# A gated mix of linear attention and a bilinear MLP: six buffers for w_down rows, attention rows loaded a unit sooner, first loads in another order

## The chip, the cores and the metric

The kernel runs on one core of a Trainium2 chip. The core has five engines with an instruction queue each, which meet only through semaphores: TensorE (PE in the profile; its weight loads are PEld) multiplies matrices, VectorE (DVE) and ScalarE (ACT) work on elements, GpSimd (POOL) here only prepares constants and issues DMAs, and SyncE (SP) issues most DMAs. Sixteen DMA engines move the data between HBM and the on-chip memory SBUF. TensorE writes to PSUM, of which the kernel uses eight tiles (banks) of 128 x 512 float32.

The metric is the device time of one execution in microseconds (us). The kernel before takes 608.49 us, the median of three runs (607.94 to 609.02).

## The reference

The input x has 2048 rows of 512. Two branches read it, and a gate per row mixes them:

```python
g = sigmoid((x * gate_w).sum(-1, keepdims=True))
a = linear_attention(x, wqkv, wo)        # 32 heads of 16
h = (x @ w_gate) * (x @ w_up)            # 2048 x 1792, no nonlinearity
b = h @ w_down
out = g * a + (1 - g) * b
```

The linear attention takes phi(t) = (t + 1 where t > 0, else exp(t)) + 1e-6 of q and k, sums kv = phi(k)^T v and z = sum of phi(k) over all rows for each head, and gives o = (phi(q) kv) / (phi(q) z + 1e-6), which is multiplied by wo. Everything is float32.

## The kernel before

**Three matmuls for one.** TensorE's fast format (float32r) keeps fewer bits than float32. So an operand is split into a high part (a rounded copy, made on ScalarE) and a low part (the difference, made on VectorE), and `mm3` issues three matmuls per product: high x high, high x low, low x high. In names the last letter tells the part: xah and xal, dh and dl, wch and wcl.

**Phase 1** reads x tile by tile (16 tiles of 128 rows), computes phi(k) and accumulates G = x^T phi(k) in PSUM. At its start all comes from HBM at once: four loads `wraw` of the key weights (`raw_load`, one of 128 rows each) and five loads `xlead` of the first four tiles of x. `wraw` is split into wkh and wkl, `xlead` into xah and xal, and the first matmul `pk<-wkh,xah` needs the first of each. TensorE meanwhile runs seven warm-up matmuls on zeros. Later tiles come as `xraw` and `xtraw`. From its sixth tile on, phase 1 also loads the first blocks of phase 2 (`cb_load` into `cbs`, three buffers): `plan(t, ...)` sets after which tile a step stands in the queues.

**Phase 2** runs over two pairs of column blocks of x (1024 rows each). For each pair there are 16 *units*: 14 for the 14 column blocks of w_gate and w_up ("f"), and two for q ("q"), at places 6 and 11. So units are numbered 0 to 31, with q at 6, 11, 22 and 27. Each unit computes two 256 x 1024 products at once by a scheme with seven products in place of eight (after Strassen and Winograd): operands are sums of blocks of x (`xc`, seven of them) and of blocks of weights (seven slots of `wr`). Products 2, 3, 4, 1, 5, 6, 7 follow one another on TensorE, into four PSUM banks Y, X, R, S; between them ScalarE copies m and cross out, and VectorE combines them. Each product is six matmuls of 128 x 512.

**The weights of a unit** come in two steps. `w_load` issues on SP a 640 KB load `wr<-in_wgu` (or in_wq). `w_add` then negates two of its blocks on ScalarE (`wr<-wr`) and issues from POOL a DMA that adds a second array from HBM onto five slots (`wr<-in_wgu_add`). `w_high` makes three copies wch on ScalarE, `w_low` three differences wcl on VectorE. In unit n, `w_high(n + 1)`, `w_low(n + 1)` and `w_add(n + 2)` run, and at its end `w_load(n + 3)`; `wr` has two buffers.

**The blocks of x for pair 1** are prepared in units 0 to 15: `cb_load`, `x_add`, `cb_split`, which writes the high and low parts to HBM (`xpark`). In unit 15, each product that has read its block for the last time lets SP load the block of pair 1 over it (`reload`): 14 loads of 512 KB, named xah<-xpark2h, xal<-xpark2l, xbh<-xpark3h and so on, in the order of the products. Unit 16 is the first to use them.

**The down projection.** An f unit leaves h split in `hh`, `hl`, and splits its rows of w_down into `dh`, `dl` (`down_tiles`, five buffers of each). Two units give eight jobs (`down_jobs`): six matmuls each into a bank `pdn`, followed by an update of `acc` on ScalarE or VectorE. A unit runs three to eight jobs from the list at four places between its products (`share`).

**The attention** of a q unit n (`attention`) goes on in the units after it. In n + 1 the terms of the denominator are written to HBM and read back, in n + 3 the reciprocal goes to HBM (`den`), and four loads `rb<-den` spread it over the heads: two at place "m" of n + 3, two at its end. In n + 3 and n + 4, `norm_high` multiplies on VectorE (`rb<-phq,rb`), ScalarE copies hh, and `norm_low` makes hl. The group then acts like two f units, with W' = kv x wo in the place of w_down. W' was computed in units 3 and 4 and parked in HBM (`wpark`); `weights` loads four tiles of 256 KB of it into buffers of dh and dl.

**What sets the order.** Nothing is scheduled: every engine runs its instructions in the order in which the program issues them (`pin`, `keep_in_program_order`). `later(n, place, fn)` adds a step to unit n at a named place; the places follow one another as e, m, c, d, t, s, r, end. The framework adds the waits. A tile pool hands out a free buffer, and its first writer waits for the last reader of the tile before. DMAs from SP use eight semaphores in turn, so in the built program the issue of a load waits for the landing of the eighth load before it.

Of the kernel before, what the change touches and what calls it, by code (L numbers as in the profile page):

```python
# [14 lines left out]
P = 128  # L15
# [28 lines left out]
def gated_mix(ctx: ExitStack, tc, xt, xp, x, wqkv, wq, wq_add, wo, wgu, wgu_add, wdn, gate_w, out):  # L44
# [12 lines left out]
    def act(dst, src, func=AF.Copy, **kw):  # L57
        pin(nc.scalar.activation(dst, src, func, **kw))  # L58
# [22 lines left out]
    def dma(dst, src):  # L81
        tc.keep_in_program_order(nc.sync.dma_start(dst, src))
# [58 lines left out]
    def w_add(n):  # L141

        if n < len(order):
            _, kind, m = order[n]
            act(raws[n][:, 5:7], raws[n][:, 0:2], scale=-1.0)
            dma_add(raws[n][:, 2:7], (wgu_add if kind == "f" else wq_add)[m])
# [32 lines left out]
    with tc.tile_pool(name="p1", bufs=2, reuse_waits="tile") as p1:  # L179
# [18 lines left out]
        def raw_load(k, by):  # L198
            pin(by.dma_start(raw_of[k], wqkv[k * P:(k + 1) * P, D:2 * D]))

        raw_load(0, nc.scalar)

        act(ezcol[:, 0:1], epsc)
        raw_load(1, nc.scalar)
        for k in range(KT):
            raw = raw_of[k]
            a = p1.tile([P, LEAD, P], F32, tag="xtraw", name="xlead", bufs=4)
            step = LEAD // 2 if k == 0 else LEAD
            for i in range(0, LEAD, step):
                sl = slice(i * P, (i + step) * P)  # L210
                dma(a[:, i:i + step].rearrange("p t c -> p (t c)"), xp[0, A1 + k // 2][:, k % 2, sl])
                if i == 0:
                    if k > 1:
                        raw_load(k, nc.sync)
                    act(wkh[:, k], raw)
                split(xa[0][:, k, sl], xa[1][:, k, sl], a[:, i:i + step].rearrange("p t c -> p (t c)"), "dve")
                if i == 0:
                    tt(wkl[:, k], raw, wkh[:, k].bitcast(F32), ALU.subtract)
# [91 lines left out]
            cbs[i] = p1.tile([P, 2, CH], F32, tag="cbs", name="cbs", bufs=3)  # L310
            x_load(cbs[i], 0, i, slice(0, 2))

        for t, i in zip((6, 7, 9, 10, 12), (4, 1, 6, 7, 3)):
            plan(t, lambda i=i: cb_load(i))
            plan(t + 2, lambda i=i: x_add(cbs[i], 0, i, slice(0, 2)))
            plan(t + 5, lambda i=i: split(*xc[i], cbs.pop(i)))
# [48 lines left out]
    def later(n, place, fn):  # L365
        at.setdefault((n, place), []).append(fn)

    def do(n, place):
        for fn in at.pop((n, place), []):
            fn()  # L370
# [16 lines left out]
    def unit(n, quad):  # L387

        wh, wl = wcs.pop(n)
        bank = {t: psum.tile([P, CH], F32, tag=t, name=f"b{t}") for t in "YXRS"}  # L390

        def reload(i):
            if n + 1 == units:
                for src, part in zip(xpark[i], xc[i]):
                    dma(part.bitcast(F32), src)

        def product(i, to, start=False):
            for k in range(2):
                ks = slice(k * P, (k + 1) * P)
                mm3(bank[to], (wh[:, SLOT[i], ks], wl[:, SLOT[i], ks]), [v[:, k] for v in xc[i]],  # L400
                    start and k == 0, k == 1, not start)
            reload(i)

        m2 = p2.tile([P, CH], F32, tag="t", name="m2")
        cross = p2.tile([P, 2, CH], F32, tag="cross", name="cross")
        product(2, "Y", True)
        act(m2, bank["Y"])
        product(3, "X", True)

        tt(bank["R"], bank["X"], m2, ALU.subtract)  # L410
        do(n, "e")
        many = share(n)
        down(many[0])
        product(4, "Y")
        act(cross[:, 0], bank["Y"])
        do(n, "m")
        do(n, "c")
        down(many[1])
        do(n, "d")
        product(1, "R")  # L420
        t = p2.tile([P, CH], F32, tag="t", name="t")
        tt(t, bank["R"], cross[:, 0], ALU.add)
        if n:
            w_high(n + 1)
        w_add(n + 2)
        do(n, "t")
        product(5, "X")
        tt(bank["S"], t, bank["X"], ALU.subtract)
        act(cross[:, 1], bank["X"])
        if n:  # L430
            w_low(n + 1, 0)
        down(many[2])
        if quad:
            quad(1, 0, cross[:, 0])
        if n:
            w_low(n + 1, 1)
        do(n, "s")
        down(many[3])
        w_low(n + 1, 2)
        if quad:  # L440
            quad(0, 1, cross[:, 1])
        product(6, "R")
        if quad:
            quad(1, 1, bank["R"])
        else:
            hh, hl = hidden()
            tt(cross[:, 1], bank["R"], cross[:, 1], ALU.mult)
            act(hh[:, 1], cross[:, 1])
        do(n, "r")
        product(7, "S")  # L450
        if quad:
            quad(0, 0, bank["S"])
        else:
            tt(cross[:, 0], bank["S"], cross[:, 0], ALU.mult)
            act(hh[:, 0], cross[:, 0])

            for c in 1, 0:
                def low(c=c):
                    tt(hl[:, c], cross[:, c], hh[:, c].bitcast(F32), ALU.subtract)

                if n + 1 == len(order):
                    later(n, f"low{c}", low)
                else:
                    low()
            return hh, hl

    def hidden():
        return [p2.tile([P, 2, CH], F32R, tag=f"h{v}", name=f"h{v}", bufs=NH) for v in "hl"]

    def down_tiles():  # L470
        return [p2.tile([P, D], F32R, tag=f"d{v}", name=f"d{v}", bufs=NH) for v in "hl"]


    att = {}
# [51 lines left out]
    def down_jobs(pair, group, col):  # L526

        def job(i):
            t = pair * TPP + i
            c, sl = divmod(i, CH // P)  # L530
            sl = slice(sl * P, (sl + 1) * P)
            s = col[:, t:t + 1]
            first = (pair, i) not in acc
            if first:
                acc[pair, i] = p2.tile([P, D], F32, tag="acc", name="acc", bufs=8)
            else:
                left[pair, i] -= 1
            ends = not left[pair, i]

            step = D // 2 if ends and pair and i == TPP // 2 - 1 else D  # L540
            for o in range(0, D, step):
                cols = slice(o, o + step)
                banks.reverse()
                pd = psum.tile([P, D], F32, tag=banks[0], name="pdn", bufs=2)[:, 0:step]
                for j, ((hh, hl), w2) in enumerate(group() if callable(group) else group):
                    mm3(pd, (hh[:, c, sl], hl[:, c, sl]), [v[:, cols] for v in w2], j == 0, j == 1)
                a = acc[pair, i][:, cols]
                if first:
                    act(a, pd, scale=s)
                else:  # L550
                    stt(a, pd, s, a, ALU.mult, ALU.add)
                if ends:
                    to = nc.gpsimd if pair == 0 else nc.sync
                    tc.keep_in_program_order(to.dma_start(out[t * P:(t + 1) * P, cols], a))

        return [lambda i=i: job((i + TPP // 2) % TPP) for i in range(TPP)]


    def attention(pair, j, n):
        phs, group = {}, {}  # L560
        den = {}
        turns = n + 5 == units

# [37 lines left out]
        def norm(i):  # L601
            r, c = parts[i]
            if r not in group:
                group[r] = (hidden(), None)
            rb = p2.tile([P, CH], F32, tag="z", name="rb", bufs=4)
            one = there[HB * i:HB * (i + 1)].rearrange("h c t -> h (c t)")
            dma(rb, one[:, None, :].to_broadcast([HB, DH, CH]))
            den[i] = rb

        def norm_high(i):  # L610
            r, c = parts[i]
            stt(den[i], phs[r, c], EPS, den[i], ALU.add, ALU.mult)
            act(group[r][0][0][:, c], den[i])

        def norm_low(i):
            r, c = parts[i]
            hh, hl = group[r][0]
            tt(hl[:, c], den[i], hh[:, c].bitcast(F32), ALU.subtract)

        def weights():  # L620
            for r in range(2):
                d = down_tiles()
                for src, part in zip(wpark[2 * j + r], d):
                    dma(part.bitcast(F32), src)
                group[r] = (group[r][0], d)

        def last():

            where = len(jobs) if turns else 0
            jobs[where:where] = down_jobs(pair, lambda: [group[0], group[1]], gcol)  # L630

        for i in range(4):
            later(n + 1, "e", lambda i=i: z_part(i))
# [8 lines left out]
        for i, places in enumerate((((n + 3, "r"), (n + 4, "e")), ((n + 4, "m"), (n + 4, "c")),  # L642
                                    ((n + 4, "d"), (n + 4, "t")), ((n + 4, "s"), (n + 4, "r")))):
            for fn, (m, place) in zip((norm_high, norm_low), places):
                later(m, place, lambda i=i, fn=fn: fn(i))
        later(*((n + 5, "e") if turns else (n + 4, "c")), weights)
        later(n + 4, "end", last)
        return quad

# [121 lines left out]
```

## Time and profile before

| what | value |
| --- | --- |
| median of three runs | 608.49 us |
| the profiled execution | 606.16 us |
| its span, first to last instruction | 604.4 us |
| granted TensorE clock | 1.000 |
| PE busy | 598.9 us, 99% of the span |
| VectorE, ScalarE busy | 443.9 us (73%), 295.3 us (49%) |
| HBM read and written | 92.54 MB, 18.09 MB |
| DMA packets, mean rate | 111.13 MB, 184 GB/s |
| first matmul after the warm-up | 5.11 us |
| units 0, 15, 16, 31 start | 93.1, 312.3, 328.6, 562.7 us |

The profiled execution is one of its own, and its time is 2.33 us under the median of the three runs. Its span leaves out 1.8 us around the instructions. Matmuls are pipelined: a matmul is shown as 0.39 us long, but the next starts 0.227 us after it. In a timeline line, the brackets at the end give how long the engine stood idle before, and what ended that. DMA share is the mean busy share of the sixteen DMA engines.

### The profile page before, as it was taken

To read this page: it belongs to the slowest core of one execution; us is meant where nothing else is said; L and a number is where in the kernel's file an instruction comes from. 1 tells how busy PE (TensorE), PEld (TensorE's weight loads), DVE (VectorE), ACT (ScalarE), POOL (GpSimd) and SP (SyncE) were. 2 spreads that over 40 slices of the span, in tenths; PEclk is the share of its full clock that TensorE was granted. 3 is DMA by queue.
4 is the path that set the end of the run, shared out by engine and by line. 5 is a ranking of instruction groups with operands and counts; after the bars stand their busy time and mean duration, and the time that the engine had idled before them with its cause. 6 is when DMAs were issued, how large, how long until landed. Compare 5 with 4: busy or idle time off the path is not lost.

```text
span 604.4 us, 7537 instructions
## 1 busy us (share of the span) xinstructions
PE 598.9 (99%) x2657; PEld 494.2 (82%) x2657; DVE 443.9 (73%) x695; ACT 295.3 (49%) x507; POOL 46.3 (8%) x62
## 2 busy tenths in 40 slices
PE   8999999999999999999999999999999999999997
PEld 6888888888888888888888888888888888888886
DVE  6977896676776798867888666456677886668874
ACT  3855765466548543564445143553473444633310
POOL 0011100001111100110100021000000000000000
PEclk9999999999999999999999999999999999999999
DMA  8576956677868967888779975444487456552313
GB/s 290 188 212 125 293 171 161 171 186 213 226 176 203 304 162 221 239 207 235 195 189 341 384 208 170 104 106 104 89 218 174 129 176 137 175 135 63 103 35 140
DMA packets 49702, 111.13 MB, mean 184 GB/s; under 512 B 4736, under 2 KB 13952, under 8 KB 49664
## 3 DMA queue, kind: packets, MB, share of 16 engines
q1 hardware_dynamic: 41968, 81.80, 40.2%
q0 software_dynamic: 7408, 28.32, 25.2%
q10 hardware_dynamic: 288, 0.52, 0.3%
q8 instruction: 21, 0.34, 0.2%
q14 instruction: 17, 0.14, 0.1%
HBM read 92.54 MB, written 18.09 MB: 183 GB/s over the span
## 4 chain that ended last, share of the span: by engine, by line
PE 99%; DMA 1%; ACT 0%; DVE 0%; issue 0%
PE pdn L52 32%; PE bY L52 14%; PE bR L52 14%; PE bX L52 14%; PE pk L52 7%; PE gt L52 7%; PE bS L52 7%; DMA wraw<-in_wqkv 1%; PE pkv L52 1%; PE pw L52 0%; PE pz L52 0%; ACT wkh L58 0%; DVE acc L64 0%
## 5 line engine op out<-in xcount | busy, mean ns | idle before, releaser
L52 PE MATMUL pdn<-dl,hh 128*128 128x512 f32 x290 | 112.4, 388 | 0.0
L52 PE MATMUL pdn<-dh,hh 128*128 128x512 f32 x290 | 112.4, 388 | 0.0
L52 PE MATMUL pdn<-dh,hl 128*128 128x512 f32 x290 | 112.4, 388 | 0.0
L58 ACT ACTIVATE hh<-cross 128x512 fp32r<-128x512 f32 x56 | 35.1, 633 | 98.2 <-DVE cross L61 98.2
L64 DVE SCALAR_TENSOR_TENSOR acc<-pdn,ocol,acc 128x512 f32<-128x512 f32 (+1 forms) x97 | 71.4, 739 | 14.9 <-PE pdn L52 13.5
L61 DVE TENSOR_TENSOR wcl<-wr,wch 128x512 fp32r<-128x512 f32 (+1 forms) x96 | 72.9, 772 | 0.0
L52 PEld LDWEIGHTS pdn<-dl,hh 128*128 128x128 f32 x290 | 54.4, 188 | 11.3
L52 PEld LDWEIGHTS pdn<-dh,hh 128*128 128x128 f32 x290 | 54.4, 188 | 11.2
L52 PEld LDWEIGHTS pdn<-dh,hl 128*128 128x128 f32 x290 | 54.4, 188 | 11.1
L58 ACT ACTIVATE wch<-wr 128x512 fp32r<-128x512 f32 (+1 forms) x96 | 60.2, 693 | 1.0 <-DMA wr<-in_wgu_add 1.0
L58 ACT ACTIVATE cross<-bY 128x512 f32<-128x512 f32 x32 | 19.1, 598 | 73.8 <-PE bY L52 60.1
L61 DVE TENSOR_TENSOR dl<-wdr,dh 128x512 fp32r<-128x512 f32 x28 | 19.4, 692 | 44.0 <-ACT dh L58 44.0
L52 PE MATMUL bX<-xbl,wch 128*128 128x512 f32 x128 | 49.9, 390 | 0.0
L52 PE MATMUL bX<-xbh,wch 128*128 128x512 f32 x128 | 49.8, 389 | 0.0
L52 PE MATMUL bX<-xbh,wcl 128*128 128x512 f32 x128 | 49.8, 389 | 0.0
L85 POOL DMA_DIRECT2D wr<-in_wgu_add x28 | 24.2, 865 | 293.4 <-ACT wr L58 138.7
L61 DVE TENSOR_TENSOR hl<-cross,hh 128x512 fp32r<-128x512 f32 x56 | 37.8, 688 | 2.7
L61 DVE TENSOR_TENSOR bR<-bX,m 128x512 f32<-128x512 f32 x32 | 22.3, 698 | 17.3 <-PE bX L52 17.3
L58 ACT ACTIVATE cross<-bX 128x512 f32<-128x512 f32 x32 | 19.1, 596 | 31.1 <-DVE bS L61 31.1
L61 DVE TENSOR_TENSOR bS<-t,bX 128x512 f32<-128x512 f32 x32 | 22.2, 695 | 14.0 <-PE bX L52 13.8
L64 DVE SCALAR_TENSOR_TENSOR acc<-pdn,gcol,acc 128x512 f32<-128x512 f32 x32 | 23.8, 749 | 10.9 <-PE pdn L52 10.7
L61 DVE TENSOR_TENSOR t<-bR,cross 128x512 f32<-128x512 f32 x32 | 22.0, 686 | 10.9 <-PE bR L52 10.9
(151 smaller groups left out, 1257.3 us busy)
## 6 DMA issues: line engine op xcount, KB each, us to landing
wr<-in_wgu SPq DMA_DIRECT2D x28, 640.0 KB, 5.7
wr<-in_wgu_add POOLq DMA_DIRECT2D x28, 640.0 KB, 7.1
wdr<-in_wdn SPq DMA_DIRECT2D x28, 256.0 KB, 2.9
xraw<-in_x SPq DMA_DIRECT2D x16, 256.0 KB, 6.2
terms<-zq SPq DMA_DIRECT2D x16, 256.0 KB, 2.2
zt<-terms SPq DMA_DIRECT2D x16, 256.0 KB, 6.3
rb<-den SPq DMA_DIRECT2D x16, 256.0 KB
cbs<-in_xp SPq DMA_DIRECT2D x14, 256.0 KB, 6.0
```

Source lines behind the costliest of these rows:

```text
L52: tc.keep_in_program_order(nc.tensor.matmul(*args, **kw))
L58: pin(nc.scalar.activation(dst, src, func, **kw))
L61: pin(nc.vector.tensor_tensor(dst, a, b, op=op))
L64: pin(nc.vector.scalar_tensor_tensor(dst, a, scalar, b, op0=op0, op1=op1))
L85: tc.keep_in_program_order(nc.gpsimd.dma_start(dst, src, accum_op=ALU.add))
```

## The change

The change has five parts.

- *Buffers.* `down_tiles` has six buffers (NH + 1), `cross` two. The room comes from the descriptor scratch, of which the program reserves 8192 bytes per partition in place of the framework's default of 16384.
- *W' rows.* `weights` stands in unit n + 3 at place "c" for all four groups. Before, it stood in unit n + 4 at "c", and for the group of unit 11 in unit n + 5 = 16 at "e". On SP's queue the four loads of unit 6's group now stand after xpark1l and before cbs, wr and the last two rb loads; those of unit 11's group after xpark7l and before wr, two rb loads and the fourteen reloads.
- *w_add.* It stands ahead of product 1 in its unit: on ScalarE the negation is now ahead of the three copies of `w_high`.
- *First loads.* `xlead` is read from the array xt, in pieces of 128 columns, not from xp. The second `wraw` goes from ACT's queue to SP's, and the tiny activation on ezcol is gone.
- *Phase 1.* One cb_load moves from tile 10 to 11, with its x_add and its split.

TensorE's instructions and their order stay the same.

```diff
         raw_load(0, nc.scalar)
-
-        act(ezcol[:, 0:1], epsc)
-        raw_load(1, nc.scalar)
         for k in range(KT):
...
-                dma(a[:, i:i + step].rearrange("p t c -> p (t c)"), xp[0, A1 + k // 2][:, k % 2, sl])
+                dma(a[:, i:i + step], xt[i:i + step, :, k, :].rearrange("t p c -> p t c"))
                 if i == 0:
-                    if k > 1:
+                    if k:
                         raw_load(k, nc.sync)
...
-        for t, i in zip((6, 7, 9, 10, 12), (4, 1, 6, 7, 3)):
+        for t, i in zip((6, 7, 9, 11, 12), (4, 1, 6, 7, 3)):
...
-        cross = p2.tile([P, 2, CH], F32, tag="cross", name="cross")
+        cross = p2.tile([P, 2, CH], F32, tag="cross", name="cross", bufs=2)
...
         do(n, "d")
+        w_add(n + 2)
         product(1, "R")
         t = p2.tile([P, CH], F32, tag="t", name="t")
         tt(t, bank["R"], cross[:, 0], ALU.add)
         if n:
             w_high(n + 1)
-        w_add(n + 2)
...
-        return [p2.tile([P, D], F32R, tag=f"d{v}", name=f"d{v}", bufs=NH) for v in "hl"]
+        return [p2.tile([P, D], F32R, tag=f"d{v}", name=f"d{v}", bufs=NH + 1) for v in "hl"]
...
-        later(*((n + 5, "e") if turns else (n + 4, "c")), weights)
+        later(n + 3, "c", weights)
...
-    nc = bacc.Bacc("TRN2", target_bir_lowering=False, num_devices=1)
+    nc = bacc.Bacc("TRN2", target_bir_lowering=False, num_devices=1, dynamic_dma_scratch_size=8192)
```

The rest of the diff hands the group and its W' tiles to `down_jobs` in another form.

More of the change, by code (lines that the diff above doesn't have):

```diff
@@ L559, in attention @@
     def attention(pair, j, n):
-        phs, group = {}, {}
+        phs, group, wrow = {}, {}, {}
         den = {}
@@ L603, in norm @@
             if r not in group:
-                group[r] = (hidden(), None)
+                group[r] = hidden()
             rb = p2.tile([P, CH], F32, tag="z", name="rb", bufs=4)
@@ L612, in norm_high @@
             stt(den[i], phs[r, c], EPS, den[i], ALU.add, ALU.mult)
-            act(group[r][0][0][:, c], den[i])
+            act(group[r][0][:, c], den[i])
         def norm_low(i):
             r, c = parts[i]
-            hh, hl = group[r][0]
+            hh, hl = group[r]
             tt(hl[:, c], den[i], hh[:, c].bitcast(F32), ALU.subtract)
@@ L621, in weights @@
             for r in range(2):
-                d = down_tiles()
-                for src, part in zip(wpark[2 * j + r], d):
+                wrow[r] = down_tiles()
+                for src, part in zip(wpark[2 * j + r], wrow[r]):
                     dma(part.bitcast(F32), src)
-                group[r] = (group[r][0], d)
         def last():
             where = len(jobs) if turns else 0
-            jobs[where:where] = down_jobs(pair, lambda: [group[0], group[1]], gcol)
+            jobs[where:where] = down_jobs(pair, [(group[r], wrow[r]) for r in range(2)], gcol)
         for i in range(4):
```

## Prediction

> **What bounds the kernel now.** I read the page first: the span, the share of each engine, the chain.
>
> ```profile
> span 604.4 us, 7537 instructions
> PE 598.9 (99%) x2657; PEld 494.2 (82%) x2657; DVE 443.9 (73%) x695; ACT 295.3 (49%) x507; POOL 46.3 (8%) x62
> PE 99%; DMA 1%; ACT 0%; DVE 0%; issue 0%
> ```
>
> TensorE is busy for 99% and is the chain. Then its waits, all there are:
>
> ```profile
> PE warm L52 <- DVE epsc L111: 1.3, 1, 1.3
> PE pk L52 <- ACT wkh L58: 0.8, 1, 0.8
> ```
>
> After 5.11 us a matmul starts every 0.227 us, down to the last at 600.71. So the change can save only what lies ahead of 5.11, and some tenths inside; anything that comes late adds in full. The question is which supplies are already just in time. TensorE's timeline shows two places:
>
> ```profile
> 251.88 0.39 PE L52 MATMUL pdn<-dh,hl 128*128 128x512 f32 x1
> 252.31 0.50 PE L52 MATMUL bY<-xc4h,wch 128*128 128x512 f32 x1
> ...
> 341.11 0.48 PE L52 MATMUL bX<-xbl,wch 128*128 128x512 f32 x1
> 341.43 0.39 PE L52 MATMUL bX<-xbh,wcl 128*128 128x512 f32 x1
> ```
>
> At 252.31 (unit 11) a matmul starts 0.43 after the one before it: 0.2 us were lost. At 341.11 (unit 16) a weight load needed the reloaded xbl, and 0.1 was lost. Both have no spare at all. Next, the timeline of SP, which issues the loads, around the second:
>
> ```profile
> 307.91 0.38 SPq L82 DMA_DIRECT2D xpark7l<-cbs  x1
> 311.45 0.33 SPq L82 DMA_DIRECT2D wr<-in_wgu  x1
> ...
> 313.88 0.33 SPq L82 DMA_DIRECT2D xah<-xpark2h  x1
> ...
> 329.86 0.32 SPq L82 DMA_DIRECT2D xbl<-xpark5l  x1
> ...
> 337.39 0.33 SPq L82 DMA_DIRECT2D wr<-in_wgu  x1
> 338.62 0.32 SPq L82 DMA_DIRECT2D dh<-wpark2h  x1
> ...
> 341.06 0.32 SPq L82 DMA_DIRECT2D dh<-wpark3h  x1
> ```
>
> A load on SP waits until the eighth one before it has landed, so dh<-wpark3h goes out at 341.06 because xbl, eight before it, landed then: 11 us after its issue. The queue is full. By stretches (PE, PEld, DVE, ACT, POOL; clock, DMA share, GB/s):
>
> ```profile
> 307.00:311.00 4.00, 4.00 (x20) 3.30 (x19) 3.83 (x6) 0.60 (x1) 0.86 (x1) 1.00 0.61 156
> 333.00:346.00 13.00, 13.00 (x59) 10.59 (x58) 8.53 (x13) 2.89 (x5) 0.00 (x0) 1.00 1.02 403
> ```
>
> From 311 to 346 the DMA engines are at a share of 1.0 to 1.06. What the change puts into this queue ahead of xbl makes TensorE late.
>
> **The change part by part.** *W' rows sooner.* Each of the four attention groups loads four tiles dh, dl of 256 KB, 1.05 MB. For unit 11's group they now stand in unit 14 at place "c", right behind xpark7l (307.91), and so ahead of wr, the last two rb loads and all 14 reloads; before they stood at 338.62 to 342.34, behind them. Their buffers were last read by jobs that ended before 301.4, so they go out at once. Price: 1.05 MB at the 403 GB/s of 333 to 346 is 2.6 us; at the 306 GB/s of 316 to 323 it is 3.4, the upper end. The lower: 307 to 311 shows a share of 0.61, so 0.39 x 4 us x 403 = 0.63 MB might slip in unseen, leaving 0.42 MB, 1.0 us. I take 2.6: two rb loads are ahead, and while they run the share stays near 0.6 with work queued (0.59 from 226 to 231), so half of the engines have no gap to fill, and a load lands with its slowest engine. [...]
> xbl has no spare, so TensorE waits 2.6 us at unit 16's product 5 (0.5 of it already at product 3, whose xbl had 2 us of spare). The later reloads, with 2 us or more of their own, follow that delay and add nothing.
>
> The group of unit 6 moves from unit 10 to unit 9, behind xpark1l (227.46), ahead of cbs, wr and the last two rb (236.54). The third rb decides:
>
> ```profile
> 241.98 0.69 DVE L64 SCALAR_TENSOR_TENSOR rb<-phq,rb 128x512 f32<-128x512 f32 x1 [0.40 <-DMA rb<-den]
> ```
>
> VectorE waited for it, then ran without a break to 253.7. Its product of bS at 250.43 releases these on ScalarE, and m releases the matmul at 252.31:
>
> ```profile
> 251.14 0.63 ACT L58 ACTIVATE hh<-cross 128x512 fp32r<-128x512 f32 x1 [0.56 <-DVE cross L61]
> 251.68 0.58 ACT L58 ACTIVATE m<-bY 128x512 f32<-128x512 f32 x1
> ```
>
> Every us by which rb lands later is one for TensorE. Bounds: 2.6, all bytes ahead of it, and 0, all hidden, as 231 to 237 has a share of 0.85. Of the 2.6 some 0.4 fits near 236, where the share falls to 0.27 for 1 us; I take 2.2.
>
> In pair 1 the two groups move the same way, but the DMA engines have room (a share of 0.37 in 560 to 574) and VectorE never waits for an rb: bounds 0 and 1, I take 0.
>
> *w_add sooner.* ScalarE's negation (0.63, queue pace 0.53) and the POOL add move ahead of w_high's three copies (1.88). In some 30 units the copies start 0.53 later; they end 2.9 us or more before the next unit reads them (245.11 against 248.03 at the least): 0. But the negation waits for its 640 KB load, and now the copies, the move of bX and the next unit's w_low on VectorE are queued behind it. Loads that landed after the copies' start: 211.3 against 208.97, 256.4 against 255.03, 290.2 against 289.6, 461.3 against 459.2; all within the spare. And one that is not, unit 16:
>
> ```profile
> 336.66 1.88 ACT L58 ACTIVATE wch<-wr 128x512 fp32r<-128x512 f32 x3
> 347.63 0.63 ACT L58 ACTIVATE wr<-wr 128x512 f32<-128x512 f32 x1 [9.10 <-DMA wr<-in_wgu]
> ```
>
> The copies for unit 17 now come after 347.63. Negation 0.53, copy one and two 1.15, then VectorE's two subtractions, with an acc update between, 2.0: the low half is ready 3.2 to 3.7 later, at 351.0. TensorE wants it at its third matmul of unit 17, 349.16 + 0.45 = 349.6: 1.3 us. If the load comes s later, so does TensorE by the first step, and 1.3 stands. Bounds 0.5 and 2.
>
> *First loads.* xlead comes from xt in pieces of 512 B (terms, of that size, run at 343 GB/s, the first loads at 381): 1.05 MB, 0.3 us more, under a spare of 1 to 2 us in the first projections. The start is set by the first wraw (in the chain from 0.80 for 3.61, so landed at 4.41), still alone at the head of ACT's queue. Bounds: 0.9 saved (a start at 4.2, where the warm-up ends) and 0.4 lost; I take 0. The dropped 0.20 activation stood in idle time.
>
> *At nothing:* cb load at 11 (SP's wait from 39.94 to 58.56 now comes behind one more xtraw; VectorE's split moves by 3 us, and its work ahead of the last g matmuls is the same sum); two cross tiles (ScalarE's waits there end on bY, 60.1, and bS, 31.1, not on old readers); six buffers (TensorE never waits on dh, dl); the smaller scratch (POOL has at most two DMAs out).
>
> **Sum.** 2.2 + 2.6 + 1.3 = 6.1 us. The profiled execution took 606.16, of which 1.8 lie around the span; so 612.3 there. It was 2.33 under the median of 608.49: predicted 614.6.
>
> **The rivals.** *Not slower: the W' rows are hidden.* They fill the share of 0.39 (307 to 311) and 0.41 (226 to 231) left by rb, xbl and rb land as before, and the early negation finds its load sooner: 608.5. It decides if the shift at xbl stays under 0.1 us; against it speaks the 0.63 MB that fits at most. [...]
> *Half hidden:* 1.0 at xbl, 0.8 at rb and 1.3: 611.6.
> *Only the negation costs:* 1.3, 609.8.
> *More late than counted:* behind the negation bX and the acc updates also hold PSUM banks; TensorE could lose a further 2 to 4 us in unit 17: 616.6 to 618.6.
> *Faster:* the start comes at 4.2 and the tenths at 93 to 119, 252 and 341 (0.85 together) go: 606.7. It needs the first wraw to land 0.9 sooner, and every other step to be wrong.
>
> **How the numbers follow.** What a measurement can tell from no change is 0.2%, 1.2 us. All three stalls 0.42 (614.6); half hidden 0.22; negation alone 0.07, on the border, half of it slower; more than counted 0.10; hidden 0.12; faster 0.07. Slower: 0.42 + 0.22 + 0.035 + 0.10, rounded 0.78; same 0.15; faster 0.07. The range from 608.0 to 616.6 leaves out faster and most of "more than counted", 0.17.
>
> **What would show it.** TensorE's waits should have new lines: bY (unit 11) on ScalarE's m, near 254.5; bX on the xbl load, near 344; unit 17's first product on wcl or wch. SP should issue xah<-xpark2h near 317 and each reload 2.6 later against its unit's start. ScalarE's wait for in_wgu should stand ahead of wch. First matmul at 5.1. If no such wait stands there, the W' bytes were hidden and I am wrong.

## The result, and the profile after

The changed kernel takes 614.22 us, the median of six runs (613.12 to 616.3); the kernel before took 608.22 in the six runs beside them (607.05 to 609.5). The ratio is 1.0102, with a 95% interval of 1.008 to 1.0124: slower by 1%, 6.0 us. (The ratios here are those on record with their intervals; they differ by up to 0.15% from the quotients of the medians.) Predicted were 614.6 us. The total came out right; of its parts only some did, as the following shows.

The page of the changed kernel's profiled execution (613.99 us), its span, busy engines and chain:

```profile
span 612.3 us, 7533 instructions
...
PE 602.4 (98%) x2657; PEld 494.6 (81%) x2657; DVE 443.3 (72%) x695; ACT 294.8 (48%) x506; POOL 46.4 (8%) x62
...
PE 81%; DMA 9%; DVE 5%; issue 2%; ACT 1%; SPq 1%; DVEq 0%; ACTq 0%
```

The chain that was 99% TensorE now runs for 9% of the span through DMAs: somewhere TensorE stood behind a load. Its waits (us in total, times, longest):

```profile
PE bX L52 <- DMA xbl<-xpark3l: 2.9, 1, 2.9
PE warm L52 <- DVE xc1h L109: 1.3, 1, 1.3
PE bY L52 <- ACT m L58: 1.2, 1, 1.2
PE pk L52 <- ACT wkh L58: 0.6, 1, 0.6
PE gt L52 <- DVE xnl L61: 0.4, 1, 0.4
```

Two were predicted (bX on an xbl, bY on m), one was not (gt on xnl), and of unit 17's wcl there is nothing. TensorE's timeline at the largest:

```profile
332.54 0.39 PE L52 MATMUL bY<-xah,wcl 128*128 128x512 f32 x1
332.83 0.47 PE L52 MATMUL bX<-xbh,wch 128*128 128x512 f32 x1
336.20 0.80 PE L52 MATMUL bX<-xbl,wch 128*128 128x512 f32 x1 [2.90 <-DMA xbl<-xpark3l]
336.79 0.63 PE L52 MATMUL bX<-xbh,wcl 128*128 128x512 f32 x1
337.21 0.63 PE L52 MATMUL bX<-xbh,wch 128*128 128x512 f32 x1
```

This is product 3 of unit 16, not product 5. And after the wait the next matmuls start 0.427 us apart, not 0.227: from 336.2 to 338.9 each takes nearly twice its time. By stretches (PE, PEld, DVE, ACT, POOL; clock, DMA share, GB/s) the clock explains it:

```profile
333.00:336.00 3.00, 0.30 (x1) 0.00 (x0) 3.00 (x6) 0.64 (x2) 0.00 (x0) 0.94 1.10 263
336.00:339.00 3.00, 2.80 (x7) 2.25 (x8) 1.44 (x3) 1.11 (x2) 0.00 (x0) 0.50 1.00 348
339.00:342.00 3.00, 3.00 (x15) 2.48 (x14) 1.55 (x3) 0.00 (x0) 0.00 (x0) 0.99 1.04 416
```

The granted clock falls to 0.50 at 335.67, near the end of the idle time, and stays there until 339.08: six matmuls with 0.2 us extra each and a part of a seventh, 1.3 us on top of the wait.

**Where all of it went.** TensorE runs the same 2657 matmuls in the same order in every kernel of this study, so the n-th matmul can be compared across traces. The table gives, for each profiled execution, how much more time TensorE took over a stretch than in the first profile of before (us). The stretches end at the matmuls that in that profile start at 80, 130, 260, 346, 352 and 601 us; the first holds the start of the first real matmul too. All fourteen traces are in it; the kernels are told of below.

| profiled execution | head, to 80 | phase 1's end | units 3 to 11 | units 11 to 16 | unit 17's start | pair 1 | sum |
| --- | --- | --- | --- | --- | --- | --- | --- |
| before | 0 | 0 | 0 | 0 | 0 | 0 | 0 |
| before, again | -0.1 | 0.0 | 2.2 | 0.4 | 0.0 | 0.0 | 2.5 |
| changed | 0.4 | 0.65 | 1.3 | 5.0 | 0.25 | 0.3 | 7.9 |
| changed, again | 0.5 | 0.7 | 3.2 | 4.3 | 0.0 | 1.3 | 10.0 |
| W' late | -0.2 | 0.6 | 1.5 | -0.1 | 1.34 | 0.0 | 3.1 |
| W' of 11 late | 0.4 | 0.6 | 1.6 | 0.1 | 1.41 | 0.2 | 4.4 |
| add late | 0.55 | 0.7 | 1.3 | 3.0 | 0.0 | 0.0 | 5.5 |
| before + W' | -0.1 | 0.0 | 1.9 | 3.2 | 0.0 | 0.15 | 5.1 |
| before + add | 1.9 | 0.2 | 1.9 | 0.3 | 1.35 | 0.0 | 5.6 |
| before + W' + add | 2.4 | 0.1 | 1.2 | 2.35 | 1.32 | 1.55 | 9.0 |
| before + first loads | 0.1 | 0.0 | 1.25 | 0.6 | 0.0 | 0.0 | 1.95 |
| before + copied block | 1.9 | 0.6 | 0.0 | 0.2 | 0.0 | 0.15 | 2.8 |
| before, rb first | 1.7 | -0.1 | -0.4 | 0.0 | 0.0 | 0.0 | 1.2 |
| rb and first loads | 0.05 | -0.1 | -0.4 | 0.0 | 0.0 | 0.0 | -0.4 |

A single profile is one draw. The next part begins with that. The stretch of units 3 to 11 goes by one load. VectorE starts on the third rb once it has landed, at 241.98 in the first profile of before; how much later it starts in another trace, TensorE's own lateness at 130 us taken off, is the loss of that stretch within 0.1 us in ten traces. (The others are "before + add", told of below, and the two with the rb loads moved.)

### The profile page after: what moved, and what is told of

Its sections match the earlier page's. It is cut to its first block, busy times and chain, and to the rows that moved or that the text cites. A ratio compares the mean times of both kernels' runs of the same rounds, so it can differ in the third digit from the quotient of the medians.

```text
span 612.3 us, 7533 instructions
## 1 busy us (share of the span) xinstructions
PE 602.4 (98%) x2657; PEld 494.6 (81%) x2657; DVE 443.3 (72%) x695; ACT 294.8 (48%) x506; POOL 46.4 (8%) x62
## 4 chain that ended last, share of the span: by engine, by line
PE 81%; DMA 9%; DVE 5%; issue 2%; ACT 1%; SPq 1%; DVEq 0%; ACTq 0%
PE pdn L52 27%; PE bX L52 12%; PE bY L52 12%; PE bR L52 12%; PE pk L52 7%; PE bS L52 6%; PE gt L52 5%; DMA xbl<-xpark3l 2%; DMA rb<-den 2%; DMA dh<-wpark3h 1%; DMA wr<-in_wgu 1%; SPq L82 1%; DVE wcl L61 1%; DMA wraw<-in_wqkv 1%; DMA den<-den 1%
## 5 line engine op out<-in xcount | busy, mean ns | idle before, releaser
L61 DVE TENSOR_TENSOR bR<-bX,m 128x512 f32<-128x512 f32 x32 | 22.3, 698 | 16.2 <-PE bX L52 16.1
L52 PEld LDWEIGHTS bX<-xbl,wch 128*128 128x128 f32 x128 | 24.3, 190 | 8.2 <-DMA xbl<-xpark3l 3.2
```

Source lines behind the costliest of these rows:

```text
L52: tc.keep_in_program_order(nc.tensor.matmul(*args, **kw))
L61: pin(nc.vector.tensor_tensor(dst, a, b, op=op))
```

## The experiments

**1. Is the first profile of before a usual one?** Its 606.16 us lie below all other runs of that kernel (606.34 to 612.86 over the runs of this study, medians 608.2 to 608.95). Both kernels were profiled again, unchanged.

> The kernel before, unchanged, profiled a second time: its 606.16 us lie below nearly all of its other runs. Theory (the just-in-time loads vary from run to run): own time 607.5 to 610, and TensorE's wait on ScalarE's m in unit 11 grown from 0.2 to about 1.2 us, as the third rb lands later after the same queue. Rival (the head varies): unit 11 as before, but more matmuls at 0.427 us after 5.1. A third: own time near 606.2 and no new wait, so that what differs lies outside the trace.

Measured: 608.58 us, span 606.9. Of TensorE's waits, the two that lie in phase 2:

```profile
PE bY L52 <- ACT m L58: 1.8, 1, 1.8
...
PE bX L52 <- DMA xbl<-xpark5l: 0.2, 1, 0.2
```

The wait that the prediction charged to the change, bY on ScalarE's m in unit 11, stands there in the kernel before, 1.8 us of it. SP and VectorE around the third rb load of this second profile:

```profile
236.47 0.37 SPq L82 DMA_DIRECT2D wr<-in_wgu  x1
236.90 1.25 SPq L82 DMA_DIRECT2D rb<-den  x2
...
244.08 0.69 DVE L64 SCALAR_TENSOR_TENSOR rb<-phq,rb 128x512 f32<-128x512 f32 x1 [2.58 <-DMA rb<-den]
```

In the first profile the same load was issued at 236.54 and VectorE went on at 241.98 after 0.40 us. The same program, the same queue ahead of it, 0.36 us later in issue, and the load took 7.2 us where it had taken 5.4. So the first profile was a lucky one by 2 us in this place.

> The changed kernel, unchanged, profiled a second time. Theory: unit 16's one wait on xbl<-xpark3l comes again, 2.5 to 3.5 us, and where TensorE is idle for 3 us or more the granted clock is 0.5 for some 2.7 us behind it (1.5 us lost); unit 17 under 0.4; unit 11 waits 1 to 2 us, as the kernel before does in its second profile. Own time 613 to 616. Rival (the drop of the clock was an accident of that execution): the wait of 3 us without a clock of 0.5, 612.5.

Measured: 616.18 us, 0.2 above the expected range. The wait on xbl<-xpark3l came again:

```profile
PE bY L52 <- ACT m L58: 2.8, 2, 1.8
PE bX L52 <- DMA xbl<-xpark3l: 2.4, 1, 2.4
...
PE bR L52 <- DVE t L61: 1.1, 1, 1.1
PE gt L52 <- DVE xnl L61: 0.4, 1, 0.4
```

and so did the clock's drop, after a shorter gap than expected: 2.83 us from one matmul's start to the next's.

```profile
337.00:338.00 1.00, 0.74 (x3) 0.65 (x4) 0.90 (x3) 0.85 (x2) 0.00 (x0) 0.93 1.08 264
338.00:341.00 3.00, 3.00 (x8) 2.32 (x8) 1.21 (x2) 0.27 (x1) 0.00 (x0) 0.50 0.99 391
```

Here it falls a little after the restart, at 337.86, and holds for 3.41 us, eight matmuls and 1.6 us lost. Unit 17 lost nothing, as expected; that pair 1 lost 1.3 us (the second wait of bY on m, at 512.69) was not. The wait of bR on t stands at the end of unit 10 and has the cause of unit 11's: VectorE stood 3.33 us for the third rb and so came late with t.

**2. Which part makes the stalls?** The four loads of W' and the early add were undone one at a time.

```diff
-        later(n + 3, "c", weights)
+        later(*((n + 5, "e") if turns else (n + 4, "c")), weights)
```

(The jobs then fetch the W' tiles when they run, as before. The old place of unit 11's group is the start of unit 16; the expectation says unit 15.)

> The changed kernel with its W' loads back at their old places (unit 10 and 15), all else as changed. Theory (the W' bytes ahead of rb and xbl make both stalls): the waits on ScalarE's m in unit 11 (1.1 us) and on xbl in unit 16 go, with them the stretch after 336.2 at a granted clock of 0.50; TensorE's last start 6.3 us sooner than in the changed kernel, 608 to 609.5 us, within 0.2% of before. Rival (the early add of POOL does it): TensorE still waits 2 us or more in unit 16, 611.5 to 613.

Measured: 609.08 us, ratio to before 1.0002 (0.9985 to 1.002).

```profile
PE bY L52 <- ACT m L58: 1.2, 1, 1.2
PE bY L52 <- DVE wcl L61: 0.7, 1, 0.7
PE gt L52 <- DVE xnl L61: 0.4, 1, 0.4
```

The time is as the theory said and unit 16's stall is gone, with the clock's drop. But unit 11's wait stays, against the expectation: the W' loads are not needed for it. And a new line appears, bY on wcl, in unit 17. With the matmuls next to it that wait costs 1.34 us: the 1.3 that the prediction gave the negation, which the changed kernel doesn't show.

Only the group of unit 11 at its old place. (The text below counts that of unit 27 with it, but `turns` holds for unit 11 alone, so the groups of 6, 22 and 27 all stay a unit sooner.)

```diff
-        later(n + 3, "c", weights)
+        later(*((n + 5, "e") if turns else (n + 3, "c")), weights)
```

> The changed kernel with the W' loads of units 6 and 22 sooner, those of units 11 and 27 at their old places. Theory: unit 11's wait stays at 1.1 us, unit 16's goes with the 0.50 clock: 5.2 us less than the changed kernel in the trace, 609 to 610.2 us. Rival (the early add): unit 16's wait stays above 2 us, 612 to 613.

Measured: 610.43 us, ratio 1.0024 (1.0005 to 1.0044), 0.2 above the theory's range. Unit 16 stands free again (0.1), unit 17 loses 1.41. Its median lies 1.35 above that of the kernel with all W' late. In twelve runs each on one chip that is more than noise (1.4 us between the means, 95% interval 0.8 to 2.0): the W' loads of units 6, 22 and 27 cost something. Where, the two traces don't tell: the stretch with unit 11 differs by 0.15 only, pair 1 by 0.24, and the head by 0.65, which is a draw.

The negation and the POOL add back behind w_high:

```diff
-        w_add(n + 2)
         product(1, "R")
...
             w_high(n + 1)
+        w_add(n + 2)
```

> The changed kernel with the negation and the POOL add back behind w_high. Theory (bytes of W' are the cause): unit 11's 1.1 stays; unit 16 still waits on xbl, 2.4 to 2.9 us, as only the add's bytes (0.64 MB, of which a part) leave the way; the clock's drop may go if the wait is shorter; unit 17's 0.24 goes: 611.5 to 613.5 us. Rival (the early add does it): unit 16's wait under 1 us and no drop, 609.5 to 610.5.

Measured: 611.97 us, ratio 1.0058 (1.0036 to 1.0081): the time is as the theory said, the one wait of 2.4 to 2.9 us isn't there.

```profile
PE bX L52 <- DMA xbl<-xpark3l: 1.2, 1, 1.2
PE bY L52 <- DMA xc4l<-xpark4l: 0.8, 1, 0.8
...
PE bX L52 <- DMA xbl<-xpark5l: 0.2, 1, 0.2
```

W' alone makes unit 16 late, but now in three shorter waits, at products 3, 4 and 5, and no clock drops. The same from the other side, before with only the W' loads moved (with six buffers and the smaller scratch):

```diff
-        later(*((n + 5, "e") if turns else (n + 4, "c")), weights)
+        later(n + 3, "c", weights)
```

> The kernel before with only the W' loads a unit sooner (and the six buffers and the smaller scratch that this needs). Theory: the third rb 1.1 us later, so 1.1 lost at unit 11; xbl late by 2.4 to 3.4 at unit 16, with 0 to 1.5 more for a clock of 0.5 behind it: 611.7 to 614.2 us. The lower end is without the clock's drop, as the POOL add of unit 17's weights is issued later again. Rival (the early add does it): 1.1 at unit 11 and under 1 at unit 16, 609.3 to 610.3.

Measured: 612.53 us, ratio 1.005 (1.0032 to 1.0068), inside the theory's range; 3.2 us at unit 16, at products 3 and 4:

```profile
PE bX L52 <- DMA xbl<-xpark3l: 1.4, 1, 1.4
...
PE bY L52 <- DMA xc4l<-xpark4l: 1.2, 1, 1.2
```

So of the changed kernel's 5.0 and 4.3 us there, some 3 come with the W' bytes alone; the rest comes in that kernel only with the early add beside them, as one long wait in place of the short ones, and the clock behind it.

**3. The early add alone, and both parts on the kernel before.** The add:

```diff
+        w_add(n + 2)
         product(1, "R")
...
             w_high(n + 1)
-        w_add(n + 2)
```

> The kernel before with only the negation and the POOL add moved ahead of w_high. Theory: unit 17 waits 1.3 us for wcl (as with the W' loads late), unit 16 nothing; unit 11 waits 1.2 for m if the early add delays the rb loads, 0.2 if not. Against the profile of before 1.3 to 2.5 us, so 607.5 to 608.7 there; the median over the runs, where before has part of unit 11's wait already, 609.3 to 610.5 us. Rival (the negation finds its load there and costs nothing): 608.5 to 609.2, no wait on wcl.

Measured: 610.66 us, 0.2 above the theory's range, ratio 1.0017 (0.9993 to 1.004): the rival's "costs nothing" is not shut out by the time, but by the trace, where unit 17 loses 1.35 us on wcl as the theory said. Unit 11's loss, 1.9 us, has here another wait, which was in no theory: TensorE waits 1.6 us for dh<-wpark1h, W' rows at their old place. So a late W' is not free either.

The same edit together with that of "before + W'":

> The kernel before with both the W' loads and the negation with its POOL add sooner, first loads and copied block as before. Theory (the add's bytes stand ahead of the late xbl): one wait of 2.5 to 3.4 us on xbl<-xpark3l at unit 16's product 3, with the clock's drop where TensorE is idle for 3 us, none at product 4, and under 0.4 us left at unit 17: 613 to 615 us. Rival (the two parts add up): products 3 and 4 lose 3.1 together as with the W' loads alone, and unit 17 loses 1.3 as with the add alone; about 613.3.

Measured: 614.67 us, ratio 1.0092 (1.0066 to 1.0118).

```profile
PE bX L52 <- DMA xbl<-xpark3l: 0.8, 1, 0.8
PE bY L52 <- DVE wcl L61: 0.7, 1, 0.7
PE bY L52 <- DMA xc4l<-xpark4l: 0.7, 1, 0.7
```

The time is in the theory's range, but the trace takes the rival's side: products 3 and 4 wait a little each (2.35 together), and unit 17 loses its 1.32. What differs from the changed kernel's one long wait can be seen in how long the reloads took, from issue to landing. The POOL add moves 640 KB. The DMA queues of the changed kernel (packets, MB, share of the 16 engines) in the 4 us before its bytes move, 329 to 333, and in the 4 us in which they do, 333 to 337; q1 is SP's queue, q0 the add's:

```profile
q1 hardware_dynamic: 482, 1.67, 102.3%
...
q0 software_dynamic: 128, 0.63, 78.2%
q1 hardware_dynamic: 155, 0.39, 27.7%
```

The add does not stand in line behind the reloads; while it runs, SP's queue moves a quarter of what it did. The first reload that it catches takes 2 to 4 us longer than before, and those behind it up to 5:

| kernel | add issued | xbl, product 3 | xc4h | xc4l | add gets ahead of |
| --- | --- | --- | --- | --- | --- |
| before | 326.05 | 12.4 us | 11.9 | 12.0 | none of these |
| before + W' | 329.71 | 12.5 | 13.0 | 15.4 | xc4l |
| add late | 330.40 | 12.5 | 13.0 | 15.2 | xc4l |
| before + W' + add | 329.57 | 12.5 | 15.9 | 15.0 | xc4h |
| changed | 329.00 | 14.4 | 16.6 | 16.1 | xbl |
| changed, again | 330.15 | 14.2 | 16.4 | 15.9 | xbl |

xbl was issued 7.3 and 7.15 us ahead of the add in the changed kernel's two profiles, 7.15 in the kernel with both parts, 8.7 with W' alone. It looks as if a near tie decides whether the add goes ahead of xbl or of xc4h; what tips it between the changed kernel and this one isn't settled (this one has one cross buffer and the old first loads).

**4. The two small parts that were costed at nothing.** The copied block's load, step 11 for 10:

```diff
-        for t, i in zip((6, 7, 9, 10, 12), (4, 1, 6, 7, 3)):
+        for t, i in zip((6, 7, 9, 11, 12), (4, 1, 6, 7, 3)):
```

> The kernel before with only one copied block's load moved from step 10 to step 11 of phase 1. Theory: its split stands between xnl's operations, so the last g matmuls wait 0.4 to 0.5 us for xnl near 90 us; 609.2 to 609.6 us. Rival (that wait belongs to the changed head): no wait on xnl, 608.9 us.

Measured: 609.74 us, ratio 1.001 (0.9988 to 1.0031): the effect is too small for the time; in the trace the wait of gt on xnl is there, 0.63 us with its neighbours. It belongs to this part: all six traces with the load at 11 lose 0.6 to 0.7 there, all with it at 10 lose 0.2 or less. VectorE in the changed kernel (first block) and before (second):

```profile
82.45 0.69 DVE L61 TENSOR_TENSOR xnl<-xraw,xnh 128x512 fp32r<-128x512 f32 x1 [1.05 <-ACT xnh L58]
...
84.88 1.22 DVE L61 TENSOR_TENSOR xal<-cbs,xah 128x1024 fp32r<-128x1024 f32 x1
...
86.62 0.69 DVE L61 TENSOR_TENSOR xnl<-xraw,xnh 128x512 fp32r<-128x512 f32 x1
...
89.03 1.22 DVE L61 TENSOR_TENSOR xbl<-cbs,xbh 128x1024 fp32r<-128x1024 f32 x1
...
90.17 0.69 DVE L61 TENSOR_TENSOR xnl<-xraw,xnh 128x512 fp32r<-128x512 f32 x1
```

```profile
82.56 0.68 DVE L61 TENSOR_TENSOR xnl<-xraw,xnh 128x512 fp32r<-128x512 f32 x1
...
85.58 0.68 DVE L61 TENSOR_TENSOR xnl<-xraw,xnh 128x512 fp32r<-128x512 f32 x1
...
88.00 1.21 DVE L61 TENSOR_TENSOR xbl<-cbs,xbh 128x1024 fp32r<-128x1024 f32 x1
...
89.13 0.68 DVE L61 TENSOR_TENSOR xnl<-xraw,xnh 128x512 fp32r<-128x512 f32 x1
```

The xal split has moved from ahead of 82 to 84.88, between the last xnl. The work is the same sum, but it has left a place in which VectorE then stands idle (1.05 at 82.45), and the last xnl comes 1.04 later.

The first loads:

```diff
-        act(ezcol[:, 0:1], epsc)
-        raw_load(1, nc.scalar)
...
-                dma(a[:, i:i + step].rearrange("p t c -> p (t c)"), xp[0, A1 + k // 2][:, k % 2, sl])
+                dma(a[:, i:i + step], xt[i:i + step, :, k, :].rearrange("t p c -> p t c"))
                 if i == 0:
-                    if k > 1:
+                    if k:
```

> The kernel before with only the first loads changed. Theory: first projection matmul at 4.53 instead of 5.11, and 0.3 to 0.75 us given back at once, in a wait for k = 1's wkh (second wraw behind three xleads on SP) or in matmuls at 0.427 us, since the clock is granted later than the start; no wait on xnl near 90; 608.3 to 609.2 us, within 0.2% of before. Rival (a start 0.58 sooner is a gain): 608.0 to 608.4 and TensorE's phase 1 ends 0.5 sooner.

Measured: 608.35 us, ratio 0.9991 (0.9969 to 1.0013): within 0.2% as expected. The first matmul starts at 4.53 instead of 5.11, and in this trace the matmuls right behind it start 0.566 and 0.42 apart. (In the changed kernel's first profile there is a wait too, the 0.6 on wkh: the second wraw, now on SP behind three xlead loads, landed at 7.47.) Across all fourteen traces this part turns out better than expected. TensorE's timeline of the kernel with only the copied block changed, so with the old first loads:

```profile
4.95 1.22 PE L52 MATMUL pk<-wkh,xah 128*128 128x512 f32 x2 [0.52 <-ACT wkh L58]
5.97 1.05 PE L52 MATMUL pk<-wkh,xal 128*128 128x512 f32 x2
6.82 1.05 PE L52 MATMUL pk<-wkl,xah 128*128 128x512 f32 x2
7.67 1.05 PE L52 MATMUL pk<-wkh,xah 128*128 128x512 f32 x2
8.53 0.97 PE L52 MATMUL pk<-wkh,xal 128*128 128x512 f32 x2
```

Pairs of 1.05 us are matmuls at 0.427, for 0.227 at full rate: the array is at about half its rate until 9 us, and the head loses 1.9 us. With the old first loads the head column holds 0, -0.1, -0.1, 1.7, 1.9, 1.9 and 2.4, a mean of 1.1; with the new ones -0.2, 0.05, 0.1, 0.4, 0.4, 0.5 and 0.55, a mean of 0.3. So they are worth some 0.8 us on average, by seven traces against seven, with single traces up to 2.5 us apart. The runs of the two kernels of part 5, which differ by these loads alone, agree: 1.1 us between the means, 0.2 to 2.0. The likely reason, an estimate from the starts in the traces, is the shorter pause behind the warm-up (0.74 to 0.87 us between starts, against 1.1 to 1.3). The traces' records of the granted clock fit it: full clock begins at 4.58 to 6.96 us in all seven traces with the new loads; with the old ones it begins at 4.03 to 4.20 in three, ahead of the pause's end, and not before 8.80 to 10.44 in the other four. No run changes the pause alone.

The six buffers, the smaller scratch and the two cross tiles were not run alone. The kernel with W' late has all of them, and at a ratio of 1.0002 no cost of theirs shows.

**5. A version that takes out the wait.** If the third rb load makes unit 11's wait, it should go when the last two rb loads stand ahead of the 640 KB weight load:

```diff
-            later(n + 3, "m" if i < 2 else "end", lambda i=i: norm(i))
+            later(n + 3, "m" if i < 2 else "r", lambda i=i: norm(i))
```

> The kernel before with the last two rb loads of each group issued ahead of the unit's 640 KB weight load instead of behind it. Theory (the third rb's landing, which varies by 1.7 us from run to run, makes unit 11's wait, 1.8 us in a usual run): it lands 1.5 us or more sooner, the wait on ScalarE's m is 0.2 or less, and the time is 606.6 to 607.6 us, 1 to 2 us below before. Rival (the weight load is then late instead, or the wait has another cause): 608.2 to 609.2, with a wait on wcl or m.

Measured, on the kernel before: 607.84 us, ratio 0.9993 (0.9975 to 1.0011). In the trace the wait on m is gone, 0.4 us below even the lucky profile, and nothing else became late; the time is 0.7 below before, not 1 to 2, and the interval takes in no gain at all. Its profiled head lost 1.7.

And with the edit of the first loads as well:

> The same, with the changed first loads too. Theory: unit 11's wait gone as there, and the first loads within 0.4 us either way: 606.2 to 607.6 us. Rival: 608 to 609 us.

Measured: 606.46 us (605.83 to 608.72), ratio 0.9976 (0.9961 to 0.9992): faster than both kernels, by a quarter of a per cent against before. All of TensorE's waits, in a profile that is the fastest of its twelve runs:

```profile
PE warm L52 <- DVE xc1h L109: 1.3, 1, 1.3
PE pk L52 <- ACT wkh L58: 0.2, 1, 0.2
```

## Why the prediction was right, and where it was wrong

**The sum (6.1 us) agrees with the measured 6.0, by errors that cancel.** Setting the two traces of the changed kernel against those of the unchanged code at each place: units 3 to 11 lose 1.3 and 3.2, against 0, 0, 1.25 and 2.2 in the four traces that have neither W' nor the add nor the rb loads moved, so about 1.4 more; unit 16 loses 4.65 against 0.3, so 4.35 more; unit 17 0.1; phase 1's end 0.65; pair 1 0.8; the first loads give back 0.8. That makes 6.5, near the 6.0 of the medians. Predicted were 2.2, 2.6, 1.3 and three times 0: that the sums agree is luck.

**Unit 11, 2.2: the chain was right, the price of the W' loads stays open, and the starting point was wrong.** The text read the 0.2 us lost at 252.31 as the state of the kernel before ("Both have no spare at all") and the 2.33 us under the median as something to add at the end. Both come from one lucky draw: in a second profile that wait is 1.8 us, without the change, and in others the head loses about 2. So the sum counted a part of this wait twice. The chain was read rightly (rb, VectorE, m, matmul): moving only the rb loads removes the wait in both traces. But W' loads (1.9 at this place), the add (1.5, with W' late) and neither (2.2) all give much the same; the load's own time from run to run, 5.1 to 7.2 us after the same queue, is as large as the term. That the W' loads do cost something is hinted twice: by the 1.4 us of the runs above, and by the third rb's time, 6.3 to 8.7 us in the six traces with W' ahead of it, 5.1 to 7.2 in the six without. Both say some 1 us, half of the term. (Its 0.4 us of cover near 236 doesn't follow from its own row either: a share of 0.27 for 1 us leaves 0.7 free.)

**Unit 16, 2.6: the mechanism was right, place and size were not.** Without a move of the W' loads of unit 11's group, unit 16 loses 0 to 0.6 in all traces; with it, 2.35 to 5.0. The failed step is "so TensorE waits 2.6 us at unit 16's product 5 (0.5 of it already at product 3)". It moved the reloads in one block and left the POOL add where it was. Both were off. With W' alone the load of product 3 landed 3.5 and 3.8 us later against the start of unit 15 than before (19.3 and 19.5 us behind it, for 15.7), where the sum had 2.6: more than its spare of 2 by 1.5 and more. (For the choice of 2.6 over 1.0, rb's loads on half of the engines, the trace of before has this: the third rb load landed in eight updates of its semaphore, 241.21 to 241.95, with VectorE going on at 241.98; the 640 KB load ahead of it landed in sixteen, 239.72 to 240.89.) And the add runs on the same engines (78.2% of their time from 333 to 337 in the changed kernel, with 27.7% left to SP's queue); issued sooner against the reloads, it takes their bandwidth during the loads of product 3 or 4, and TensorE waits there. W' alone costs 3.0 to 3.2; behind the one long wait a granted clock of 0.50 adds 1.3 and 1.6, of which no row of before gave a sign in phase 2.

**Unit 17, 1.3: right in size, but not beside a late unit 16.** Four traces show 1.32 to 1.41 us on wcl. The changed kernel shows 0.25 and 0. The failed sentence is "If the load comes s later, so does TensorE by the first step, and 1.3 stands": the load landed 6.1 us later (353.72 for 347.63), TensorE came 7.3 later and used up the wait. With both parts on the kernel before, where TensorE came 6.1 later for the same 6.1 of the load, the 1.3 is there. In the changed kernel these two stalls in series on one supply are not a sum.

**Costed at nothing.** The copied block: 0.6, because the cover named ("its work ahead of the last g matmuls is the same sum") was idle time that doesn't come back once passed. The first loads: inside the bounds, -0.9 to +0.4, at about -0.8; the reading "still alone at the head of ACT's queue" missed that the first wraw landed 0.6 sooner (3.80 for 4.41). Pair 1: the bounds were 0 and 1, the value taken 0; the changed kernel shows 0.3 and 1.3, as VectorE there waits 1.76 us for an rb in the second profile. In the four traces in which both W' and the add come sooner in pair 1 it is 0.24 to 1.55, in the ten others 0.15 or less.

**The rivals.** "Not slower, W' hidden" fell at unit 16: 1.005 (1.0032 to 1.0068) with W' alone. In a queue that before was at a share of 1.0 to 1.06 from 311 to 346, the early issue cost 3.0 to 3.2 us. "Only the negation" is out in the changed kernel. "More late than counted" had the sign of the surprise, but named PSUM banks, and the trace shows none. "Half hidden" (611.6) and "faster" (606.7) lie below the lowest run, 613.12.

**Of what was to be seen:** bY on m near 254.5 (it stands at 254.62); bX on an xbl, though at 336.2 and not near 344; ScalarE's wait for in_wgu, 15.3 us in five for 10.3 in three before:

```profile
ACT wr L58 <- DMA wr<-in_wgu: 15.3, 5, 9.6
```

The first matmul at 5.1 (4.53), the wait on wcl and xah<-xpark2h near 317 (319.98) failed.

## What to carry to other kernels

Profile the kernel before twice before reading a spare of some tenths out of one trace: where a load is just in time, its own variation (here 2 us in 7) makes a wait that belongs to no change, and a profile that lies under the median is a hint of it. In a DMA queue at a share of 1.0, an early load was here paid for by what stood behind it (1.05 MB of W', 3.0 to 3.2 us at unit 16), and a transfer issued by another engine took from the same engines (in 4 us of the POOL add SP's queue moved 0.39 MB, for 1.67 in the 4 us before); ask which loads are on the way while such a transfer runs. Where TensorE bounds a kernel, small, urgent loads can be put ahead of a large one that has time (the rb loads ahead of the weights: the wait is gone from the trace; in the time the gain is clear only with the first loads of this change, ratio 0.9976).

## What was not expected of the hardware

- *After two idle stretches of about 3 us TensorE ran at half its rate.* After gaps of 3.37 and 2.83 us from start to start the granted clock was 0.50 for 3.41 us, once from the end of the idle time on and once from two matmuls behind it; gaps of up to 2.2 us in the other traces left it at 1.00. The length of the gap may not be all that counts: in all fourteen traces the changes of the clock lie whole multiples of 3.413 us apart (97 of them from full clock to the drop in both cases), and in the 3.413 us that ended with a drop TensorE was busy for a share of 0.23 and 0.24, estimated from the starts of its matmuls; past the start, the emptiest such stretch without a drop has 0.53. That the share of such a stretch decides is an estimate from these two drops; no run varies it.
- *The start of the kernel is a draw.* With the same first loads, 0 to 11 matmuls behind the warm-up ran at 0.427 us. The clock's column stood at 1.00 in these stretches all the same (6.0 to 9.0 of the kernel with the copied block: 9 matmuls, for 15 in 3 us at full rate). That trace's record of the clock begins only at 9.27, where the matmuls become fast; so at the start count the matmuls, and don't trust the column.
- *A load's time varies by a third.* With W' and add at their old places, the third rb load took 5.1 to 5.4 us in three traces and 7.2 in a fourth. (In the one with 5.1 it was issued 1.7 us later than in the first profile, which cost TensorE 1.25.)
